# Narrowing float64 weights to float32 inside a fused attention, expert and cosine kernel: two bit operations instead of three, low word through ScalarE and GpSimd

## The chip, the cores and the metric

One core of one Trainium2 chip runs the whole program in one launch. The metric is the time of one execution on the device, in microseconds (us); lower is better. The engines are TensorE (PE; its weight loads are PEld), VectorE (DVE), ScalarE (ACT), GpSimd (POOL) and SyncE (SP), which here only issues transfers. Each engine takes its instructions in the order of the program, and DMA engines move data between device memory and the on-chip memory (SBUF).

## What is computed

```python
# 1: attention over pairs of averaged queries, (4, 8, 1152, 64)
q_pool = q.reshape(B, H, S // 2, 2, D).mean(axis=3)
scores = scale * np.matmul(q_pool, k.transpose(0, 1, 3, 2))
attn = softmax(scores)
x = np.matmul(attn, v)             # then 2304 tokens x 512
# 2: each token goes to one of 8 experts
logits = x @ w_gate
expert_idx = np.argmax(logits, axis=1)
out[mask] = gate_w[mask, None] * (np.maximum(x[mask] @ w1[e], 0.0) @ w2[e])
# 3: a product with a cosine
h = x @ w_in                       # w_in: 512 x 2048, float64
g = h * np.cos(h)
return (g @ w_out).astype(np.float32)   # w_out: 2048 x 512, float64
```

`w_in` and `w_out` arrive as float64, 8 MB each; the engines compute in float32, so the kernel makes float32 copies of them in device memory first. That is the narrowing. A float64 is two 32-bit words: the high word has the sign, 11 bits of exponent and 20 bits of fraction, the low word 32 more bits of fraction.

## The kernel before

The program has three stages that overlap at their ends. The attention stage (to about 640 us) computes 32 heads and routes the tokens. The expert stage works through 12 units of up to 256 tokens, sorted by expert; `Experts.unit` does one. The cosine stage (`Cosine.block`) works through five blocks of up to 512 tokens.

**A unit of the expert stage.** The hidden layer is done in four chunks. For each, TensorE multiplies the tokens with a chunk of `w1` into PSUM (line 916), ScalarE takes the relu into the tile `hh` (line 922), VectorE computes the rounding remainder `hl` from the same PSUM tile (line 923), and TensorE multiplies `hh` and `hl` with a chunk of `w2` (line 955). Products are split in a high and a low part for accuracy. Two chunks are in flight (`HP = 2`). Line 983 scales the unit's result on ScalarE, line 984 copies its row numbers on VectorE. Beside this, weights of later experts are loaded by SP (line 1054), rounded on ScalarE (line 1055) and their remainder taken (line 1056) by VectorE, for the last chunk by GpSimd. GpSimd also issues the gathers of the next units' tokens (lines 1002 and 1010) and of the cosine stage's tokens (line 1030).

**The narrowing.** `Narrow.step` handles 128 rows by 256 columns. There are 64 steps, spread over the first ten units by the table `NSTEP`. A step of the kernel before:

- line 1102, SP: load 256 KB into `raw64`; `hi` and `lo` are its odd and even words;
- line 1108, VectorE: `v` = (hi shifted left by 3) xor a constant;
- line 1109, VectorE: `t` = the sign of hi;
- line 1110, VectorE: `v` = (v and a mask) or `t`;
- line 1112, ScalarE: `t` = hi squared, which says below whether the number is too small;
- line 1113, VectorE: `v` is set to zero where `t` says so;
- line 1114, VectorE: `t` = sign and exponent of `v`, a power of two;
- line 1115, VectorE: `t` = lo times 2 to the -52 times `t`, the low word's share;
- line 1116, GpSimd: `v` = `v` + `t`;
- line 1117, ScalarE's queue: store `v` to `wi_d` or `wo_d` in device memory.

The tiles `raw64`, `v64` and `t64` have four buffers each, so step n + 4 can write a buffer only when step n has read it for the last time. Since `t` is used by lines 1109 and 1110 and then overwritten by line 1112, ScalarE's square has to wait for VectorE's line 1110 of its own step.

**The order.** The code does not fix the order of one step against the rest of its unit: a scheduler orders the instructions of each engine when the program is built, and that order is kept by each engine at run time. An instruction that waits holds up all that follow on its engine.

Of the kernel before, what the change touches and what calls it, by code (L numbers as in the profile page):

```python
# [8 lines left out]
F32 = mybir.dt.float32  # L9
# [4 lines left out]
AF = mybir.ActivationFunctionType  # L14
ALU = mybir.AluOpType
# [17 lines left out]
    l=0.55, v=3.2, vc=2.8, vt=0.3, vx=0.3, n=1.1,  # L33
# [454 lines left out]
class Routing:  # L488
# [83 lines left out]
    def plan(self, at, ends, x, batch, ps, low):  # L572
# [149 lines left out]
        for j, t in enumerate(range(lo, hi)):  # L722
            at(z + 4.4 + j * step, scatter, t)
# [347 lines left out]
class Narrow:  # L1071
# [26 lines left out]
    def step(self, src, dst):  # L1098
        nc, p = self.nc, self.pool
        shape = [P, self.W]  # L1100
        raw = p.tile(shape + [2], I32, name="raw64")
        nc.sync.dma_start(raw, src)
        lo, hi = raw[:, :, 0].bitcast(U32), raw[:, :, 1]
        v = p.tile(shape, I32, name="v64")
        t = p.tile(shape, I32, name="t64")
        vf, tf = v.bitcast(F32), t.bitcast(F32)

        nc.vector.tensor_scalar(v, hi, 3, 0x40000000, op0=ALU.logical_shift_left, op1=ALU.bitwise_xor)
        nc.vector.tensor_single_scalar(t, hi, -0x80000000, op=ALU.bitwise_and)
        nc.vector.scalar_tensor_tensor(v, v, 0x7FFFFFFF, t, op0=ALU.bitwise_and, op1=ALU.bitwise_or)  # L1110

        nc.scalar.activation(tf, hi.bitcast(F32), AF.Square)
        nc.vector.scalar_tensor_tensor(vf, tf, 3.4332275390625e-05**2, vf, op0=ALU.is_ge, op1=ALU.mult)
        nc.vector.tensor_single_scalar(t, v, -0x800000, op=ALU.bitwise_and)
        nc.vector.scalar_tensor_tensor(tf, lo, 2.0**-52, tf, op0=ALU.mult, op1=ALU.mult)
        nc.gpsimd.tensor_add(vf, vf, tf)
        nc.scalar.dma_start(dst, vf)


# [73 lines left out]
def body(ctx, tc, q, k, v, w_gate, w1, w2, w_in, w_out, out):  # L1193
# [104 lines left out]
    with mid as s:  # L1298
# [15 lines left out]
        for u, (i, j, n) in enumerate(UNIT):  # L1314
# [17 lines left out]
            for k in range(NSTEP[u]):  # L1332
                between[k * NCH // NSTEP[u]].append((ORD[2 if u else 3], step))
# [87 lines left out]
```

## Time and profile before

| | |
|---|---|
| median of 3 runs | 1386.64 us (1386.04 to 1390.84) |
| the profiled execution | 1400.46 us, its span 1398.9 us |
| PE busy | 1257.8 us, 90% of the span |
| DVE busy | 1087.6 us, 78% |
| ACT busy | 715.4 us, 51% |
| POOL busy | 626.2 us, 45% |

The profile is of one execution, 1% above the median of the others. Shares over the whole span mix three stages: the narrowing runs only from about 650 to 947 us, so what counts for the change is read from that stretch alone. "Idle before" of a group of instructions is the time for which its engine stood still just ahead of them, and the name behind the arrow is what ended it.

### The profile page before, as it was taken

How to read it: one execution, taken by the hardware profiler on the slowest of the kernel's cores; microseconds unless marked ns; L12 is line 12 of the kernel's file. 1: busy time of each engine (PE TensorE's matmuls, PEld its weight loads, DVE VectorE, ACT ScalarE, POOL GpSimd, SP SyncE). 2: the span in 40 equal slices, each digit the busy share in tenths (PEclk: the TensorE clock that was granted, in tenths of full speed). 3: DMA queues.
4: the chain of work that ended last, by engine and by line, in shares of the span. 5: the costliest groups of instructions: out<-in, count | busy, mean ns of one | idle time of the engine just before them, and what ended most of it. 6: DMA issues, size and time to landing. Idle time of an engine off the chain costs nothing. (4 is left out here: it accounts for less than half of the span.)

```text
span 1398.9 us, 27350 instructions
## 1 busy us (share of the span) xinstructions
PE 1257.8 (90%) x10190; PEld 1059.8 (76%) x10190; DVE 1087.6 (78%) x2203; ACT 715.4 (51%) x1631; POOL 626.2 (45%) x559
## 2 busy tenths in 40 slices
PE   5896997999979999999699897878899999999996
PEld 4686876878868887878588786767687888888885
DVE  5996988788979998865689988796965666667674
ACT  4685875777758876873154334555322223222232
POOL 6684876566668778641354444554302002001010
PEclk8898999799989998999899998999999999999998
DMA  9449345333543342415778767887102001001000
GB/s 173 96 114 183 87 102 73 75 82 86 117 61 93 86 100 63 114 32 98 175 253 251 230 196 242 264 251 220 45 0 63 1 0 61 1 8 38 0 31 16
DMA packets 126910, 146.23 MB, mean 105 GB/s; under 512 B 35888, under 2 KB 83120, under 8 KB 126768
## 3 DMA queue, kind: packets, MB, share of 16 engines
q1 hardware_dynamic: 108784, 114.97, 33.0%
q0 software_dynamic: 5600, 15.25, 3.6%
q10 hardware_dynamic: 12384, 14.17, 3.3%
q8 instruction: 82, 1.34, 0.4%
q14 instruction: 60, 0.49, 0.1%
HBM read 97.57 MB, written 28.43 MB: 90 GB/s over the span
## 5 line engine op out<-in xcount | busy, mean ns | idle before, releaser
L319 POOL TENSOR_TENSOR pl<-pf,ph 128x576 f16<-128x576 f32 x220 | 311.6, 1425 | 138.9 <-ACT ph L309 57.3
L297 ACT ACTIVATE pf<-pst 128x288 f32<-128x288 f32 x576 | 222.5, 419 | 100.5 <-PE pst L289 81.0
L263 DVE TENSOR_REDUCE mm<-pm 128x1 f32<-128x384 f32 x432 | 226.7, 545 | 44.0 <-PE pm L254 36.7
L288 PE MATMUL pst<-q,k 128*128 128x288 f32 x576 | 197.0, 349 | 0.6 <-ACT pf L297 0.4
L289 PE MATMUL pst<-q,k 66*128 66x288 f32 x576 | 173.5, 310 | 25.4 <-DMA q<-mx 25.4
L338 PE MATMUL po<-va,pl 128*128 128x66 f16 (+1 forms) x1440 | 180.3, 198 | 1.8 <-DVE pl L319 1.0
L336 PE MATMUL po<-va,ph 128*128 128x66 f16 (+1 forms) x1440 | 181.7, 199 | 0.2 <-ACT pe L342 0.2
L337 PE MATMUL po<-va,ph 128*128 128x64 f16 (+1 forms) x1440 | 179.4, 197 | 0.0
L482 POOL DMA_INDIRECT out_dram<-os,token x18 | 18.2, 1012 | 353.2 <-ACT os L1186 186.2
L254 PE MATMUL pm<-k,q 128*128 128x384 f32 x384 | 153.3, 418 | 18.1 <-DVE mm L263 14.8
L1157 ACT ACTIVATE a<-a,hpi 128x512 f32<-128x512 f32 (+1 forms) x80 | 54.5, 681 | 210.9 <-DVE a L1156 197.9
L336 PEld LDWEIGHTS <-ph 128*128 128x128 f16 (+1 forms) x1440 | 137.8, 103 | 25.5 <-issue 11.0
L338 PEld LDWEIGHTS <-pl 128*128 128x128 f16 (+1 forms) x1440 | 139.3, 103 | 15.1 <-issue 6.0
L337 PEld LDWEIGHTS <-ph 128*128 128x128 f16 (+1 forms) x1440 | 139.5, 102 | 7.9 <-issue 2.7
L289 PEld LDWEIGHTS pst<-q,k 66*128 66x128 f32 x576 | 114.5, 200 | 27.7 <-DMA q<-mx 18.6
L309 ACT CAST ph<-pf 128x576 f16<-128x576 f32 x191 | 129.5, 680 | 1.4 <-PE po L337 0.4
L1147 PE MATMUL ch<-zh,w1h_m 128*128 128x512 f32 (+1 forms) x320 | 119.6, 374 | 3.5 <-ACTq L1370 3.4
L1147 PE MATMUL ch<-zl,w1h_m 128*128 128x512 f32 (+1 forms) x320 | 119.6, 374 | 0.0
L1147 PE MATMUL ch<-zh,w1l_m 128*128 128x512 f32 (+1 forms) x320 | 119.0, 372 | 0.0
L288 PEld LDWEIGHTS pst<-q,k 128*128 128x128 f32 x576 | 114.1, 199 | 5.8 <-ACT pf L297 2.1
L1171 PE MATMUL po<-w2h_m,gh 128*128 128x512 f32 x288 | 114.2, 396 | 0.0
L1171 PE MATMUL po<-w2l_m,gh 128*128 128x512 f32 x288 | 113.8, 395 | 0.0
(262 smaller groups left out, 3331.6 us busy)
## 6 DMA issues: line engine op xcount, KB each, us to landing
w1r_e<-in_moe_w_dram SPq DMA_DIRECT2D x32, 512.0 KB
w2r_e<-in_moe_w_dram SPq DMA_DIRECT2D x32, 512.0 KB
kr<-in_k_dram SPq DMA_DIRECT2D x32, 288.0 KB
vr<-in_v_dram SPq DMA_DIRECT2D x32, 288.0 KB
k<-k SPq DMA_DIRECT2D x32, 288.0 KB
q<-q SPq DMA_DIRECT2D x60, 144.0 KB
qr<-in_q_dram SPq DMA_DIRECT2D x32, 256.0 KB
raw<-in_moe_w_in_dram SPq DMA_DIRECT2D x32, 256.0 KB
```

The lines of the kernel that those rows point to most:

```text
L254: nc.tensor.matmul(ps[:, :384], self.st[i]["q1"][:, q0 : q0 + P], self.st[i]["k1"][:, ks], start=True, stop=True)
L263: self.nc.vector.tensor_reduce(self.mm[i % 2][:, ci, g : g + 1], self.st[i]["pm", ci, g][:, :384], axis=AX.X, op=ALU.max)
L288: nc.tensor.matmul(ps[:, :288], s["k1"][:, ks], s["q1"][:, o], start=True, stop=False)
L289: nc.tensor.matmul(ps[:, :288], self.k2[i % 3][: D + 2, ks], self.q2[i % 4][: D + 2, o], start=False, stop=True)
L297: nc.scalar.activation(s["pf", c][:, j * 288 : (j + 1) * 288], s["pst", c, j][:, :288], AF.Exp, scale=0.0625)
L309: nc.scalar.copy(ph, pf)
L319: low = eng.tensor_sub(s["pl"][:, c, :], s["pf", c], s["ph"][:, c, :])
L336: nc.tensor.matmul(po[:, :66], hi, va[:, c, D:130], start=(c == 0), stop=False)
L337: nc.tensor.matmul(po[:, :D], hi, va[:, c, :D], start=False, stop=False)
L338: self.product = nc.tensor.matmul(po[:, :66], lo, va[:, c, D:130], start=False, stop=(c == NK - 1))
L1147: nc.tensor.matmul(ph[:, :n], wt[:, c, fs], z[:, c, :n], start=(k == 0), stop=(k == 3 * NDC - 1))
L1171: nc.tensor.matmul(po[j], g[:, ts], wt[:, f % FC, :], start=(f == 0 and k == 0), stop=(f == NFC2 - 1 and k == 2))
```

## The change

Sign and exponent are now made by two operations of VectorE, and `t` is no longer needed there. A new tile `l64`, again with four buffers, takes the low word, scaled by ScalarE; GpSimd multiplies it with the power of two and then adds it. In the changed kernel the lines are: 1108 and 1111 the two bit operations, 1113 the square, 1114 the setting to zero, 1116 the scaling on ScalarE, 1117 the power of two, 1118 the multiplication on GpSimd, 1119 the addition, 1120 the store.

```diff
-        nc.vector.tensor_scalar(v, hi, 3, 0x40000000, op0=ALU.logical_shift_left, op1=ALU.bitwise_xor)
-        nc.vector.tensor_single_scalar(t, hi, -0x80000000, op=ALU.bitwise_and)
-        nc.vector.scalar_tensor_tensor(v, v, 0x7FFFFFFF, t, op0=ALU.bitwise_and, op1=ALU.bitwise_or)
+        nc.vector.tensor_scalar(
+            v, hi, 3, 0x3FFFFFFF, op0=ALU.logical_shift_left, op1=ALU.bitwise_and
+        )
+        nc.vector.scalar_tensor_tensor(v, hi, -0x40000000, v, op0=ALU.bitwise_and, op1=ALU.bitwise_or)
 
         nc.scalar.activation(tf, hi.bitcast(F32), AF.Square)
         nc.vector.scalar_tensor_tensor(vf, tf, 3.4332275390625e-05**2, vf, op0=ALU.is_ge, op1=ALU.mult)
+        l = p.tile(shape, F32, name="l64")
+        nc.scalar.activation(l, lo, AF.Copy, scale=2.0**-52)
         nc.vector.tensor_single_scalar(t, v, -0x800000, op=ALU.bitwise_and)
-        nc.vector.scalar_tensor_tensor(tf, lo, 2.0**-52, tf, op0=ALU.mult, op1=ALU.mult)
-        nc.gpsimd.tensor_add(vf, vf, tf)
+        nc.gpsimd.tensor_mul(l, l, tf)
+        nc.gpsimd.tensor_add(vf, vf, l)
         nc.scalar.dma_start(dst, vf)
```

The scheduler orders the expert stage anew. Three places follow; a number behind a name is only that of a buffer or of an instruction.

VectorE, second unit, before: from the remainder of its first chunk (`hl_u_0`) to that of its second (`hl_u_1`). Line 1108 there begins the fifth step and needs the `v` of the first.

```order
L923 SCALAR_TENSOR_TENSOR hl_u_0_12579<-ph_u_0_12553,hh_u_0_12578 128x512
L1115 SCALAR_TENSOR_TENSOR t_12425<-raw_12422,t_12425 128x256
...
L1115 SCALAR_TENSOR_TENSOR t_12462<-raw_12459,t_12462 128x256
L1109 TENSOR_SCALAR t_12499<-raw_12496 128x256
L1108 TENSOR_SCALAR v_12498<-raw_12496 128x256
L816 TENSOR_REDUCE ext<-ge 128x8
L850 SCALAR_TENSOR_TENSOR seg<-count_u,size 128x12
L923 SCALAR_TENSOR_TENSOR hl_u_1_12608<-ph_u_1_12582,hh_u_1_12607 128x512
```

VectorE, the same place now:

```order
L923 SCALAR_TENSOR_TENSOR hl_u_0_12584<-ph_u_0_12558,hh_u_0_12583 128x512
L818 COPY cum<-ext 128x8
...
L820 TENSOR_TENSOR cum<-cum,ext 128x1
L923 SCALAR_TENSOR_TENSOR hl_u_1_12613<-ph_u_1_12587,hh_u_1_12612 128x512
...
L853 COPY rows<-yx 128x8
L1108 TENSOR_SCALAR v_12502<-raw_12500 128x256
```

The fifth step's first operation has moved from ahead of the second chunk's remainder to behind the third's; only small operations of the routing are left between the first two.

ScalarE, sixth unit, before, from the last weight rounding ahead of its first relu (`hh_u_0`) to its third:

```order
L1055 CAST w2h_e_3_13813<-w2r_e_3_13815 128x1024
...
L1117 DMA wo_d<-v_13465 128x256
L1112 ACTIVATE t_13722<-raw_13719 128x256
L922 ACTIVATE hh_u_0_13914<-ph_u_0_13889 128x512
L922 ACTIVATE hh_u_1_13943<-ph_u_1_13918 128x512
L1117 DMA wo_d<-v_13642 128x256
L1117 DMA wo_d<-v_13655 128x256
L1112 ACTIVATE t_13735<-raw_13732 128x256
L922 ACTIVATE hh_u_2_13972<-ph_u_2_13947 128x512
```

ScalarE, the same place now:

```order
L1120 DMA wo_d<-v_13802 128x256
L983 ACTIVATE ys_u_0_13880<-py_u_0_13545,gate_e_1_13204 128x512
L1116 ACTIVATE l_14031<-raw_14023 128x256
...
L1055 CAST w2h_e_3_13846<-w2r_e_3_13848 128x1024
...
L922 ACTIVATE hh_u_0_13949<-ph_u_0_13924 128x512
L1113 ACTIVATE t_14040<-raw_14037 128x256
L922 ACTIVATE hh_u_1_13978<-ph_u_1_13953 128x512
```

The square and the store that stood right ahead of the unit's first relu are gone from there. A square now depends on its load and on the `t` of four steps before, no longer on VectorE's work in its own step; a scaling (line 1116) depends on its load and on the `l` of four steps before.

GpSimd, around the first gather of the cosine stage's tokens, before (the row ahead of it is the 54th addition):

```order
L1116 TENSOR_TENSOR v_14795<-v_14795,t_14796 128x256
L1030 DMA yg_15672<-y_d,source 128x513
L1056 TENSOR_TENSOR w1l_e_3_15149<-w1r_e_3_15150,w1h_e_3_15148 128x1024
L1032 COPY token<-yg_15672 128x1
L1116 TENSOR_TENSOR v_14832<-v_14832,t_14833 128x256
```

GpSimd, the same place now (the row ahead of the gather is the 64th and last addition):

```order
L1118 TENSOR_TENSOR l_15500<-l_15500,t_15495 128x256
...
L1119 TENSOR_TENSOR v_15494<-v_15494,l_15500 128x256
L1118 TENSOR_TENSOR l_15538<-l_15538,t_15533 128x256
L1119 TENSOR_TENSOR v_15532<-v_15532,l_15538 128x256
L1030 DMA yg_15736<-y_d,source 128x513
L1056 TENSOR_TENSOR w1l_e_3_15208<-w1r_e_3_15209,w1h_e_3_15207 128x1024
```

All 64 steps now lie ahead of that gather on GpSimd, and on ScalarE all 64 stores lie ahead of the first relu of the tenth unit, where 54 did.

## Rows read from the trace of the kernel before

**Rows 1.** Stretches: length; busy us (instructions) of PE, PEld, DVE, ACT, POOL; PE's clock; DMA.

```profile
650.00:905.00 255.00, 218.51 (x1302) 190.86 (x1302) 209.85 (x517) 103.19 (x169) 121.84 (x98) 0.91 0.73 218
905.00:950.00 45.00, 34.60 (x186) 29.37 (x186) 36.58 (x66) 21.34 (x36) 24.21 (x22) 0.89 0.78 244
...
1000.00:1387.00 387.00, 383.60 (x1771) 315.15 (x1770) 261.37 (x467) 109.26 (x182) 28.77 (x36) 1.00 0.06 19
```

**Rows 2.** Chain of work that ended last, its shares of the span by line.

```profile
by line: PE ch L1147 11.3%; PE po L1171 11.2%; PE pt_y L1065 0.3%; POOLq L1417 0.1%; ACTq L1417 0.1%; POOL out_dram L482 0.1%; issue 0.0%; ACT os L1186 0.0%; POOLq L482 0.0%; ACTq L1186 0.0%
```

**Rows 3.** Who waited for whom: PE, 640 to 1000 us (total, times, longest).

```profile
PE py_u L955 <- DVE hl_u L923: 17.7, 9, 4.6
PE py_u L955 <- ACT hh_u L922: 16.9, 4, 7.5
```

**Rows 4.** Groups of instructions, 640 to 950 us: busy us, mean ns | idle before.

```profile
L1116 POOL TENSOR_TENSOR v<-v,t 128x256 f32<-128x256 f32 x64 | 70.3, 1105 | 89.1 <-DVE t L1115 60.7 <-issue 17.0 <-DMA wi_d<-v 3.1
...
L1113 DVE SCALAR_TENSOR_TENSOR v<-t,v 128x256 f32<-128x256 f32 x64 | 39.0, 617 | 4.7 <-ACT t L1112 4.7
L1115 DVE SCALAR_TENSOR_TENSOR t<-raw,t 128x256 f32<-128x256 uint32 x64 | 35.8, 570 | 0.2
...
L1110 DVE SCALAR_TENSOR_TENSOR v<-v,t 128x256 int32<-128x256 int32 x64 | 32.4, 518 | 0.2
...
L1112 ACT ACTIVATE t<-raw 128x256 f32<-128x256 f32 x64 | 27.1, 436 | 96.1 <-DVE v L1110 84.0 <-POOL v L1116 6.5 <-DMA wo_d<-v 5.2
...
L1114 DVE TENSOR_SCALAR t<-v 128x256 int32<-128x256 int32 x64 | 24.1, 385 | 0.0
...
L1109 DVE TENSOR_SCALAR t<-raw 128x256 int32<-128x256 int32 x64 | 20.5, 322 | 10.7 <-DMA raw<-in_moe_w_out_dram 5.8 <-DMA raw<-in_moe_w_in_dram 4.3 <-POOL v L1116 0.6
L1108 DVE TENSOR_SCALAR v<-raw 128x256 int32<-128x256 int32 x64 | 19.3, 307 | 22.6 <-DMA wi_d<-v 13.2 <-DMA wo_d<-v 9.3
```

**Rows 5.** Timeline of GpSimd, VectorE, ScalarE and PE, 786 to 792 us (start, us).

```profile
787.29 2.36 POOL L1056 TENSOR_TENSOR w2l_e<-w2r_e,w2h_e 128x1024 fp32r<-128x1024 f32 x1
...
786.76 3.19 DVE L1113 SCALAR_TENSOR_TENSOR v<-t,v 128x256 f32<-128x256 f32 x1
...
792.48 0.67 DVE L923 SCALAR_TENSOR_TENSOR hl_u<-ph_u,hh_u 128x512 fp32r<-128x512 f32 x1
...
790.31 0.43 ACT L1112 ACTIVATE t<-raw 128x256 f32<-128x256 f32 x1 [4.41 <-DVE v L1110]
...
791.28 0.79 PE L955 MATMUL py_u<-w2h_e,hh_u 128*128 128x512 f32 x1 [5.36 <-ACT hh_u L922]
```

**Rows 6.** Timeline of VectorE and PE, 847 to 853 us.

```profile
847.99 3.85 DVE L1110 SCALAR_TENSOR_TENSOR v<-v,t 128x256 int32<-128x256 int32 x1
...
852.85 0.79 PE L955 MATMUL py_u<-w2h_e,hh_u 128*128 128x512 f32 x1 [7.52 <-ACT hh_u L922]
```

**Rows 7.** Timeline of VectorE and PE, 676 to 678 us.

```profile
676.16 0.33 DVE L1108 TENSOR_SCALAR v<-raw 128x256 int32<-128x256 int32 x1 [5.10 <-DMA wi_d<-v]
...
677.84 0.79 PE L955 MATMUL py_u<-w2h_e,hl_u 128*128 128x512 f32 x1 [4.59 <-DVE hl_u L923]
```

**Rows 8.** A short stretch, columns as in rows 1.

```profile
791.30:796.30 5.00, 4.30 (x9) 2.96 (x10) 4.73 (x14) 0.98 (x3) 2.67 (x3) 0.50 0.64 176
```

**Rows 9.** Who waited for whom: SP's DMA queue, 640 to 960 us.

```profile
SPq L1102 <- DVE t L1115: 97.0, 37, 11.0
```

**Rows 10.** Groups of instructions, 640 to 950 us: rounding of w2 on ScalarE.

```profile
L1055 ACT CAST w2h_e<-w2r_e 128x1024 fp32r<-128x1024 f32 x29 | 30.3, 1046 | 25.2 <-DMA w2r_e<-in_moe_w_dram 13.3 <-POOL v L1116 10.4 <-PE py_u L955 0.9
```

**Rows 11.** Instructions of lines 1116 and 1117: ns min/median/max, first and last start.

```profile
L1116 POOL TENSOR_TENSOR v<-v,t x64: 717/818/4145, 660.2 to 945.1; 128x256 f32<-128x256 f32 x64
...
L1117 ACTq DMA_DIRECT2D wi_d<-v x32: 326/326/451, 661.0 to 879.4; - x32
L1117 ACTq DMA_DIRECT2D wo_d<-v x32: 326/326/358, 749.0 to 946.7; - x32
```

**Rows 12.** Timeline of ScalarE: the first relu of the tenth unit.

```profile
906.95 0.60 ACT L922 ACTIVATE hh_u<-ph_u 128x512 fp32r<-128x512 f32 x1
```

## The prediction

> **What bounds the kernel now.** I read the table by stretches first, to see in which part of the program TensorE stands still. From 1000 us on, in the cosine stage, it is busy 383.6 of 387 us at full clock [rows 1], and the chain of work that ended last is made there of its matmuls alone [rows 2]. So a microsecond by which that stage starts earlier or later moves the end by one. The narrowing runs ahead of it. From 650 to 905 us TensorE is idle for 255 - 218.5 = 36.5 us, from 905 to 950 us for 10.4, and its clock is granted to 0.91 and 0.89 [rows 1]. Those 47 us, with the clock lost around them, are all the change can win at once; VectorE is the fullest of the helpers, 209.9 of 255 us.
>
> Then I asked who ends TensorE's waits: the relu of ScalarE, 16.9 us in 4 waits, and the remainder of VectorE, 17.7 in 9 [rows 3]. Neither is long work; both stand in a queue behind something else. The groups by line say what: ScalarE stood still for 84.0 us ahead of its squares because VectorE had not done line 1110 [rows 4]. The timelines show the coupling at its worst. GpSimd subtracts a weight chunk for 2.36 us; VectorE's line 1113 takes 3.19 us beside it; ScalarE stands 4.41 us ahead of the square, with the relu queued behind it, and TensorE stands for 5.36 us [rows 5]. The same happens at 853 us, with line 1110 held 3.85 us and TensorE 7.52 [rows 6]. At 678 us VectorE itself waits 5.10 us for a free `v`, with a remainder queued behind it: 4.59 us of TensorE [rows 7].
>
> **The change, part by part.** *VectorE.* Line 1109 goes, 64 x 0.322 = 20.6 us, and line 1115, 64 x 0.570 = 36.5 [rows 4]: 57.1 us less. The new second bit operation reads two tiles as line 1110 did, so it stands at 0.518, at nothing net. *ScalarE* gains 64 scalings. The nearest row is the square, same shape, same spacing of the source: 64 x 0.436 = 27.9 us [rows 4], on an engine busy 103.2 of 255 us [rows 1], beside waits that hide it. *GpSimd* gains 64 multiplications. The nearest row is line 1116, of equal shape: 0.717 at least, 1.105 on average, 4.145 at most [rows 4, 11]; I take the mean, 70.7 us. Beside GpSimd's 121.8 of 255 us [rows 1] this has room, but not much (below). The other bit operation and the stores keep their price.
>
> *Waits that go.* (a) At 678 us the remainder now stands ahead of the fifth step, as the second extract in the part on the change shows: 4.6 us gone. (b) The square no longer needs VectorE, so at 791 and 853 us the relu runs early: 5.36 + 7.52 = 12.9 us are at stake. But the remainder, which TensorE needs right after, was itself only done at 793 us [rows 5], on a VectorE that still stops for GpSimd's 2.36. Between nothing and 12.9 I take half, 6.4. (c) From 905 us on no narrowing is left in the new order, where ten stores were still to come: half of the 10.4 us idle there, 5.2; the rest waits for weights. (d) The clock: from 791.3 to 796.3 us, right behind a wait, it was granted at 0.50 (the 1.2 GHz level), and 4.30 us of matmuls [rows 8] would have taken half at the upper level: 2.15 us lost. One such loss for (a), and half of two for (b): 4.3. Together 20.5 us.
>
> *Waits that come.* (e) Stores and scalings on ScalarE's queue both wait for GpSimd. Such waits stood at 10.4 us ahead of the w2 rounding [rows 10] and 6.5 ahead of a square [rows 4]; with twice the work per step on GpSimd I let them double, 16.9 us more of ScalarE. In the new order 13 of 40 relus stand directly behind a store or a scaling (9 before), so 13/40 of it reaches TensorE: 5.5 us, between 0 and 16.9. (f) The narrowing is packed closer: 64 stores ahead of the tenth unit's first relu, at 906.95 us [rows 12], where 54 stood. What is left of the idle time before 905 us, 36.5 - 4.6 - 6.4 = 25.5 us, grows with its density, by 10/54: 4.7 us; it could be none, since SP waited 97.0 us to reload `raw` until line 1115 had read it [rows 9], and the scaling now frees `raw` sooner.
>
> The sum: 20.5 - 5.5 - 4.7 = 10.3 us less. On the profiled execution that is 1400.5 - 10.3 = 1390.2; the median of the runs lies 13.8 us lower, and I take the same difference from it: **1376.3 us**, 0.7% faster. About 0.5%, some 7 us, is what a measurement of this kernel can tell from no change.
>
> **The rivals.** *The wait changes its name (no change).* VectorE's remainder is as late as before, since its long holds come from GpSimd, which now multiplies as well. Then (b) is nothing, (c) too, only (a) and its clock are won: 4.6 + 2.15 - 5.5 - 4.7 = -3.4, so 1390. For it: 17.7 us of TensorE's waits end with the remainder already [rows 3], and the denser order gives VectorE's relief back to the narrowing. Against it: even if each multiplication held VectorE for a whole 0.717, that is 45.9 us, less than the 57.1 it is rid of.
>
> *GpSimd ends last (slower).* In the new order ScalarE cannot take the tenth unit's first relu before all 64 additions, and the first gather of the cosine stage stands behind them on GpSimd. The first store was issued at 661.0 us, the last at 946.7 [rows 11]: 4.5 us a step, where now 3.9 are needed. GpSimd's other work from 650 to 905 us is 121.8 - 54 x 1.105 = 62.2 us [rows 1, 4], so 128 operations have 193 us: the queue is full when their mean reaches 1.5 us. At 1.7 it ends 62.2 + 128 x 1.7 - 255 = 24.8 us late; less (a) and (c), 9.8, the kernel takes 1402, and above a mean of 1.64 it is slower by over 0.5%. For it: the same operation took from 0.717 to 4.145 us [rows 11], and VectorE and GpSimd hold each other up: line 1113 ended 0.3 us after GpSimd's subtraction [rows 5]. Against it: VectorE leaves as many such operations as GpSimd takes up, and 1.105 would have to become 1.5. The Trainium skill (SBUF — State Buffer, "SBUF: two separate sides") speaks for this rival: VectorE and GpSimd share a port pair under an exclusive lock, held for a whole instruction, when VectorE works with two SBUF inputs or in a two-port mode. By that rule the moved multiplication still takes the pair once per step, and the change frees no port time. The trace agrees on the block itself, 3.19 us beside 2.36; that the sum of the holds is the limit no row shows.
>
> **How the numbers follow.** The forecast case has 0.47, with a range of its own from 1363 to 1380: down to all of (b) and (c) with the clock of both waits, 24 us; up to the smallest gain that counts. No change has 0.32, GpSimd last 0.21: the order shows its condition, but only a mean a third higher would meet it. So faster 0.47, same 0.32, slower 0.21. The range for all is 1363 to 1397: below it a tenth or less of the first case, above it somewhat more than half of the last.
>
> **What would show it.** Right: ScalarE's 84 us ahead of the square gone; VectorE's busy time from 650 to 950 us down by 30 us or more; the waits at 791 and 853 us shorter than 3; the last store ahead of 915 us; no narrowing beside units ten to twelve. The first rival: TensorE's wait for the remainder above 20 us while that for the relu falls below 8. The second: lines 1118 and 1119 at 1.5 us or more on average, ScalarE waiting for line 1119 for over 40 us, and the tenth unit's first relu behind 907 us. Wrong altogether: a stop that none of these names, as weights that land late because ten more steps load beside them; ScalarE's 13.3 us for w2 [rows 10] would then grow past 25.

## The result and the profile after

The change makes the kernel slower: 1396.3 us (median of 15 runs, 1392.2 to 1405.6) against 1387.5 for the kernel before beside it, a ratio of 1.0070 with a 95% interval of 1.0048 to 1.0092. The forecast was 1376.3. The profiled execution took 1404.3 us with a span of 1402.7, again one near the top of its runs, so it stands fairly beside that of before (1400.5 and 1398.9).

The stretches of the profile after come first, with the columns of [rows 1]: length, busy time of TensorE, its weight loads, VectorE, ScalarE, GpSimd, then clock and DMA. The second block is the kernel before, from 650 to 950 us.

```profile
650.00:905.00 255.00, 208.83 (x1222) 181.34 (x1221) 210.29 (x424) 122.36 (x227) 171.11 (x167) 0.89 0.75 219
905.00:950.00 45.00, 37.28 (x228) 33.10 (x227) 22.19 (x30) 21.91 (x31) 19.65 (x14) 0.92 0.74 226
1000.00:1391.00 391.00, 387.53 (x1786) 318.01 (x1785) 264.69 (x473) 111.02 (x184) 28.91 (x37) 1.00 0.06 18
...
650.00:950.00 300.00, 246.11 (x1448) 214.43 (x1447) 232.49 (x453) 144.27 (x258) 190.76 (x180) 0.90 0.75 220
```

```profile
650.00:950.00 300.00, 253.12 (x1486) 220.22 (x1486) 246.43 (x583) 124.52 (x203) 146.05 (x119) 0.91 0.74 222
```

The cosine stage is unchanged, full from start to end. From 905 to 950 us TensorE gained 37.28 - 34.60 = 2.7 us, but from 650 to 905 us it lost 218.51 - 208.83 = 9.7, and its clock went from 0.91 to 0.89. The odd number is VectorE's: 128 operations fewer are asked of it in the narrowing, and it is as busy as before, 210.3 against 209.9 us. In part that is because seven more steps lie ahead of 905 us (63 of 64, where 56 did); but over 650 to 950 us, where all the narrowing lies, it is only 13.9 us less busy, where the prediction looked for 30 or more. The groups by line, 640 to 950 us, say why (busy us, mean ns | idle time before and what ended it):

```profile
L1118 POOL TENSOR_TENSOR l<-l,t 128x256 f32<-128x256 f32 x64 | 60.3, 949 | 55.9 <-DVE t L1117 42.1 <-DVE gate_e L1016 4.0 <-ACT w1h_e L1055 3.3
L1119 POOL TENSOR_TENSOR v<-v,l 128x256 f32<-128x256 f32 x64 | 58.4, 921 | 1.9
L1114 DVE SCALAR_TENSOR_TENSOR v<-t,v 128x256 f32<-128x256 f32 x64 | 39.5, 622 | 1.0
L1111 DVE SCALAR_TENSOR_TENSOR v<-raw,v 128x256 int32<-128x256 int32 x64 | 38.6, 610 | 0.5
...
L1117 DVE TENSOR_SCALAR t<-v 128x256 int32<-128x256 int32 x64 | 32.8, 520 | 0.5
...
L1108 DVE TENSOR_SCALAR v<-raw 128x256 int32<-128x256 int32 x64 | 29.7, 470 | 17.2 <-DMA wi_d<-v 9.8 <-issue 3.8 <-POOL l L1118 1.2
...
L1113 ACT ACTIVATE t<-raw 128x256 f32<-128x256 f32 x63 | 27.2, 435 | 62.3 <-POOL l L1118 33.2 <-DMA raw<-in_moe_w_in_dram 16.2 <-DMA raw<-in_moe_w_out_dram 5.5
L1116 ACT ACTIVATE l<-raw 128x256 f32<-128x256 uint32 x63 | 26.7, 432 | 15.9 <-POOL v L1119 14.2 <-issue 1.7
```

Each VectorE operation that stayed got longer. The second bit operation takes 610 ns where line 1110 took 518, the power of two 520 where line 1114 took 385, the first bit operation 470 where line 1108 took 307 [rows 4]. A step's four operations sum to 0.470 + 0.610 + 0.622 + 0.520 = 2.22 us; the six of before summed to 2.72. ScalarE's 84 us of waiting for VectorE's bits are gone, and 33.2 + 14.2 us of waiting for GpSimd have come.

What this does to TensorE, in the waits of 640 to 1000 us (total, times, longest):

```profile
PE py_u L955 <- DVE hl_u L923: 15.5, 6, 8.4
PE py_u L955 <- ACT hh_u L922: 11.2, 5, 3.8
PE py_u L955 <- DVE ys_u L984: 9.8, 3, 5.1
PE pt_e L1065 <- DMA xg_e<-x_d,ix_e: 7.4, 4, 4.3
PE phT_u L944 <- ACT hs_u L938: 6.1, 2, 6.0
```

The copy of line 984 stands next to the remainder on VectorE and feeds no matmul, so its 9.8 us belong to the remainder: 25.3 us, where [rows 3] had 17.7. Of the 25.3, one stop of 8.4 us, at 671 us, is no work of VectorE's that was stretched: VectorE waits there for a store to land. Without it, and without the 4.6 us at 678 us of before [rows 7], where VectorE waited for a store too, the remainder went from 13.1 to 16.9 us. The relu fell from 16.9 to 11.2, gathers and the small units' relu rose from 1.9 and 2.6 before to 7.4 and 6.1. The two waits of before:

```profile
PE phT_u L944 <- ACT hs_u L938: 2.6, 1, 2.6
PE pt_e L1065 <- DMA xg_e<-x_d,ix_e: 1.9, 1, 1.9
```

One of the remainder's waits in full, from the timeline of VectorE, GpSimd and TensorE:

```profile
856.97 0.74 POOL L1119 TENSOR_TENSOR v<-v,l 128x256 f32<-128x256 f32 x1
...
857.06 4.38 DVE L1117 TENSOR_SCALAR t<-v 128x256 int32<-128x256 int32 x1
...
858.24 2.36 POOL L1056 TENSOR_TENSOR w2l_e<-w2r_e,w2h_e 128x1024 fp32r<-128x1024 f32 x1
...
860.54 0.74 POOL L1118 TENSOR_TENSOR l<-l,t 128x256 f32<-128x256 f32 x1
...
861.36 0.68 DVE L923 SCALAR_TENSOR_TENSOR hl_u<-ph_u,hh_u 128x512 fp32r<-128x512 f32 x1
...
862.09 0.80 PE L955 MATMUL py_u<-w2h_e,hl_u 128*128 128x512 f32 x1 [4.38 <-DVE ys_u L984]
```

The power of two needs 0.28 us alone. It was issued while GpSimd added, and ended only when GpSimd had added, subtracted a weight chunk and multiplied: 4.38 us, the remainder right behind it, and TensorE still for 4.38 us. Who is held, and who is not, is plain in two lines' shortest, median and longest times (ns):

```profile
L1117 DVE TENSOR_SCALAR t<-v x64: 277/286/4377, 654.6 to 908.2; 128x256 int32<-128x256 int32 x64
L923 DVE SCALAR_TENSOR_TENSOR hl_u<-ph_u,hh_u x40: 677/682/694, 633.1 to 929.8; 128x512 fp32r<-128x512 f32 x40
```

Line 923, which reads one tile from PSUM and one from SBUF, never took more than 694 ns in this run, whatever GpSimd did. The operations that read SBUF alone are stretched, those with one tile like those with two. The Trainium skill (SBUF — State Buffer, "SBUF: two separate sides") has it so: VectorE with two SBUF inputs, or in a two-port mode, and GpSimd exclude each other on one port pair, for a whole instruction. The trace agrees (which mode line 1117 ran in no row tells), and shows one thing more, that the one who waits can be passed over by several of the other's instructions in a row.

To compare kernels I count this **hold**: over 650 to 950 us, each narrowing operation and weight subtraction on VectorE that the timeline lists singly and that lies beside a tensor operation of GpSimd, its duration less what it takes alone (0.285 us with one tile read, 0.415 with two, 1.22 for a weight chunk, near the medians of such lines). Rows that the timeline merges into one are left out, so it is a count from below. Before it is 39.6 us in 110 instructions, after 59.3 in 145. Outside such company the same operations come to 2.2 us over their time alone at most, in sum, in any of the kernels here.

### The profile page after: what moved, and what is told of

It reads as the page before. It is cut to its first block, busy times and chain, and to the rows that moved or that the text cites. A ratio compares the mean times of both kernels' runs of the same rounds, so it can differ in the third digit from the quotient of the medians.

```text
span 1402.7 us, 27424 instructions
## 1 busy us (share of the span) xinstructions
PE 1254.3 (89%) x10190; PEld 1056.0 (75%) x10190; DVE 1071.0 (76%) x2075; ACT 738.3 (53%) x1695; POOL 673.4 (48%) x623
## 3 DMA queue, kind: packets, MB, share of 16 engines
q1 hardware_dynamic: 108784, 114.97, 33.1%
## 5 line engine op out<-in xcount | busy, mean ns | idle before, releaser
L338 PEld LDWEIGHTS <-pl 128*128 128x128 f16 (+1 forms) x1440 | 138.2, 102 | 15.1 <-issue 5.8
```

The source lines that it names most:

```text
L338: self.product = nc.tensor.matmul(po[:, :66], lo, va[:, c, D:130], start=False, stop=(c == NK - 1))
```

## The experiments

Theories: **A**, VectorE is held by GpSimd's additional work; **B**, raw tiles come free earlier and their loads collide with the units' transfers; **C**, ScalarE waits for GpSimd. All runs together:

| kernel | us | ratio to before (95%) | hold, us |
|---|---|---|---|
| before | 1387.5 | 1 | 39.6 |
| the change | 1396.3 | 1.0070 (1.0048, 1.0092) | 59.3 |
| e1_bits | 1383.1 | 0.9944 (0.9916, 0.9972) | 35.3 |
| e2_low | 1396.2 | 1.0033 (1.0008, 1.0058) | 53.5 |
| e3_dvemul | 1386.8 | 0.9963 (0.9934, 0.9992) | 28.7 |
| e4_nomul | 1389.6 | 0.9993 (0.9965, 1.0022) | 36.5 |
| e5_wdve | 1389.3 | 0.9987 (0.9968, 1.0006) | 39.3 |
| e6_mul2 | 1414.5 | 1.0164 (1.0132, 1.0197) | 74.5 |
| e7_raw3 | 1399.0 | 1.0062 (1.0039, 1.0085) | 54.2 |
| e8_adddve | 1367.7 | 0.9833 (0.9800, 0.9866) | 21.2 |
| e9_idlepool | 1399.0 | 1.0088 (1.0054, 1.0121) | 54.0 |
| e10_handoff | 1396.8 | 1.0048 (1.0018, 1.0078) | 16.8 |
| e11_bits_dve | 1378.0 | 0.9923 (0.9895, 0.9950) | 24.2 |
| e12_before_dve | 1374.0 | 0.9904 (0.9872, 0.9935) | 24.1 |
| e13_five | 1393.5 | 1.0040 (1.0023, 1.0058) | 61.1 |
| e14_hand5 | 1378.2 | 0.9917 (0.9891, 0.9943) | 26.0 |
| e15_dve5 | 1374.1 | 0.9908 (0.9874, 0.9942) | 17.5 |
| e16_dve_w | 1370.8 | 0.9859 (0.9831, 0.9887) | 3.4 |

The kernel before was run beside each group of four and had medians of 1387.5 to 1391.1, so kernels of different groups are compared by their ratios. Through the table the ratio rises with the hold, from 0.986 at 3.4 us to 1.016 at 74.5. A straight line through the other seventeen misses none of them by more than 0.8% and e10_handoff by 1.6%; its slope is 0.6 us of time for 1 us of hold, an estimate from these rows.

**The halves.** e1_bits is the kernel before with the two bit operations alone:

```diff
-        nc.vector.tensor_scalar(v, hi, 3, 0x40000000, op0=ALU.logical_shift_left, op1=ALU.bitwise_xor)
-        nc.vector.tensor_single_scalar(t, hi, -0x80000000, op=ALU.bitwise_and)
-        nc.vector.scalar_tensor_tensor(v, v, 0x7FFFFFFF, t, op0=ALU.bitwise_and, op1=ALU.bitwise_or)
+        nc.vector.tensor_scalar(
+            v, hi, 3, 0x3FFFFFFF, op0=ALU.logical_shift_left, op1=ALU.bitwise_and
+        )
+        nc.vector.scalar_tensor_tensor(v, hi, -0x40000000, v, op0=ALU.bitwise_and, op1=ALU.bitwise_or)
```

> Theories. A (the shared pair of ports): GpSimd's new multiplication holds VectorE's remaining operations, so the remainder is as late as before and VectorE's stretch 650 to 905 us stays at 210 us. B (earlier reloads): the raw tile comes free sooner, so its loads run beside the units' stores, token gathers and weights, and TensorE waits for these. C (ScalarE waits on GpSimd): the squares and scalings that wait for t and l (33 + 14 us) hold the relu and the weight casts. This run is the bit half alone; the low word stays with VectorE and GpSimd has one addition, so nothing of A, B or C is in it: all three expect no loss, 1378 to 1388 us beside 1387.5 before, VectorE's busy time in 650 to 905 us down by 20 us or more. If it is above 1392, all three fall and the cause lies in the order of the steps that the shorter VectorE work brings.

Measured 0.6% faster, as all three had it, with the hold at 35.3 us; only VectorE's busy time did not fall (208.5 us), since more of the narrowing now lies in that stretch. The other half by itself, e2_low, has the three bit operations and the new low word:

```diff
-        nc.vector.scalar_tensor_tensor(tf, lo, 2.0**-52, tf, op0=ALU.mult, op1=ALU.mult)
-        nc.gpsimd.tensor_add(vf, vf, tf)
+        l = p.tile(shape, F32, name="l64")
+        nc.scalar.activation(l, lo, AF.Copy, scale=2.0**-52)
+        nc.gpsimd.tensor_mul(l, l, tf)
+        nc.gpsimd.tensor_add(vf, vf, l)
```

> The low-word half alone: three bit operations on VectorE, the scaling on ScalarE, the multiplication and addition on GpSimd. A: the loss is here, 1394 to 1404 us, and VectorE's busy time in 650 to 905 us goes above 210 us (64 operations more than in the full change). B: here as well, 1392 to 1400, with waits for token gathers as after. C: here as well. If it is within 1384 to 1390, the loss comes only from both halves together.

It is slower, and its hold is 53.5 us. The loss sits in the low word's half; VectorE's busy time did rise, to 212.9. The halves do not add up: -0.6% and +0.3% make -0.2%, where the change has +0.7%. The order of the queues differs in each of the three, and what that is worth comes below.

**GpSimd's multiplication.** In e3_dvemul it goes to VectorE, in e4_nomul it is left out, in e6_mul2 it is there twice; the rest is the change.

```diff
-        nc.gpsimd.tensor_mul(l, l, tf)
+        nc.vector.tensor_mul(l, l, tf)
```

> The full change but the multiplication on VectorE, so that GpSimd has one addition a step as before and t is freed by VectorE. A: the loss goes, 1380 to 1389 us; the bit operations L1108 and L1111 and the power of two L1117 fall back to 0.31, 0.52 and 0.39 us on the mean. B: the raw tile is free as early as in the change, so the loss stays, 1393 to 1399. C: the squares no longer wait for GpSimd, most of the loss goes, 1382 to 1390, whatever VectorE's means are.

```diff
-        nc.gpsimd.tensor_mul(l, l, tf)
         nc.gpsimd.tensor_add(vf, vf, l)
```

> The full change with GpSimd's multiplication left out (the scaled low word is added without its power of two). A: 1376 to 1388 us and VectorE's busy time in 650 to 905 us 20 us or more below the 210 of the change. B: the raw tile is free as early as in the change, so 1392 to 1398 with the same waits for gathers and stores. C: 1380 to 1388, with ScalarE's wait on GpSimd (33 + 14 us) under 20.

```diff
         nc.gpsimd.tensor_mul(l, l, tf)
+        nc.gpsimd.tensor_mul(l, l, tf)
         nc.gpsimd.tensor_add(vf, vf, l)
```

> The change with a second GpSimd multiplication of the same size in each step (the low word is multiplied twice, so its value differs). From no multiplication to one, the time went from 1389.5 to 1396 us. A: the dose goes on, another 6 to 14 us: 1402 to 1412, time of VectorE beside GpSimd above 75 us over its time alone. B: the raw tile comes free no earlier and no later, so 1394 to 1400. C (ScalarE waits for GpSimd): also longer, 1402 to 1415, but then with ScalarE's wait on GpSimd going from 47 us to over 80 while VectorE's time beside GpSimd stays near 60.

No multiplication on GpSimd 0.9993, one 1.0070, two 1.0164: each costs 0.8 to 0.9%, some 11 to 13 us. The groups by line of e4_nomul, then of e6_mul2, between which GpSimd's two multiplications are the whole difference:

```profile
L1111 DVE SCALAR_TENSOR_TENSOR v<-raw,v 128x256 int32<-128x256 int32 x64 | 33.8, 535 | 0.3
```

```profile
L1111 DVE SCALAR_TENSOR_TENSOR v<-raw,v 128x256 int32<-128x256 int32 x61 | 50.6, 836 | 0.7
...
L1113 ACT ACTIVATE t<-raw 128x256 f32<-128x256 f32 x60 | 26.1, 436 | 54.7 <-POOL l L1119 49.5 <-DVE v L1114 2.3 <-DVE hl_u L923 2.2
L1116 ACT ACTIVATE l<-raw 128x256 f32<-128x256 uint32 x58 | 24.4, 433 | 38.5 <-POOL v L1120 33.1 <-DVE xl_e L1068 3.2 <-issue 2.0
```

The bit operation goes from 535 over 610 to 836 ns on VectorE, while its hold goes 36.5, 59.3, 74.5. The hold missed its mark of 75 by a hair, but ScalarE's waits for GpSimd grew as well, to 49.5 + 33.1 us, so the dose does not part A from C; e9_idlepool below does. B is out as the main cause: in e3_dvemul and e4_nomul the raw tile is free as early as in the change, and they are not slower than before. In e3_dvemul the three means fell to 0.38, 0.53 and 0.37 us, the first not as far as A had said; in e4_nomul VectorE's busy time fell to 186.3, as it had.

**Fewer loads ahead**, e7_raw3, tests B itself, and **less other work on GpSimd**, e5_wdve, tests A without touching the steps.

```diff
-        raw = p.tile(shape + [2], I32, name="raw64")
+        raw = p.tile(shape + [2], I32, name="raw64", bufs=3)
```

> The change with three raw tiles instead of four, so that a step's load is issued one step later and fewer loads stand beside the units' stores and gathers; no engine's work changes. B: most of the loss goes, 1385 to 1391 us, and TensorE's waits for token gathers (7.4 us) and the wait for the store of the first unit (13.5 us on VectorE) go. A: 1394 to 1402, not better, since VectorE is held as before.

```diff
-        ws[i].append(weight_chunk(nc, wp[i % 2], wp["raw"], w1[number[i]], w2[number[i]], c, f"e{i}_{c}", (c == NCH - 1 and (i > 0 or E0P),) * 2))
+        ws[i].append(weight_chunk(nc, wp[i % 2], wp["raw"], w1[number[i]], w2[number[i]], c, f"e{i}_{c}", (False,) * 2))
```

> The change with the weights' subtractions of each last chunk on VectorE instead of GpSimd. A (VectorE is held beside GpSimd's work; in the change its five narrowing and subtraction groups spend 60 us more beside it than alone): GpSimd loses 34 us of work in 650 to 905 us, VectorE gains 14 x 1.22 = 17 us of its own, the time beside GpSimd falls below 45 us: 1388 to 1396 us. B (earlier reloads collide with the units' transfers): untouched, 1394 to 1400. If VectorE's own amount of work sets the time, 1398 to 1406.

e7_raw3 is no faster than the change, though TensorE's waits for gathers fell from 7.4 to 3.3 us and VectorE's longest wait for a unit's store from 13.5 to 2.4: B falls. e5_wdve, where a step passes through GpSimd as in the change, is back within the error of before, 0.8% faster than the change, with 20 us less hold although VectorE took on 14 weight subtractions. GpSimd's busy time fell by only 16 us there (171.1 to 155.3), since steps moved up into the stretch.

**Nothing of the step on GpSimd**, e8_adddve:

```diff
-        nc.gpsimd.tensor_mul(l, l, tf)
-        nc.gpsimd.tensor_add(vf, vf, l)
+        nc.vector.tensor_mul(l, l, tf)
+        nc.vector.tensor_add(vf, vf, l)
```

> The change with the multiplication and the addition both on VectorE, so that GpSimd has nothing of a step but its gathers and weights. A: VectorE's time beside GpSimd falls to 15 us over its time alone or less, against 64 x 0.42 = 27 us of additions that it takes on: about even with the multiplication alone on VectorE (1386.8), 1380 to 1390. If VectorE's own amount of work sets the time, as the prediction had it, 10 to 20 us above that run: 1394 to 1406.

1367.7 us, faster than both kernels and than either theory allowed; the hold, at 21.2 us, is above the 15 that A had said. Six operations a step on VectorE, and TensorE is busy 227.1 of 255 us, as the groups by line and the stretch show:

```profile
L1111 DVE SCALAR_TENSOR_TENSOR v<-raw,v 128x256 int32<-128x256 int32 x64 | 33.3, 528 | 0.0
L1114 DVE SCALAR_TENSOR_TENSOR v<-t,v 128x256 f32<-128x256 f32 x64 | 30.7, 485 | 0.0
...
L1118 DVE TENSOR_TENSOR l<-l,t 128x256 f32<-128x256 f32 x64 | 28.0, 446 | 0.0
L1119 DVE TENSOR_TENSOR v<-v,l 128x256 f32<-128x256 f32 x64 | 27.5, 436 | 0.1
...
L1117 DVE TENSOR_SCALAR t<-v 128x256 int32<-128x256 int32 x64 | 22.6, 362 | 0.0
L1108 DVE TENSOR_SCALAR v<-raw 128x256 int32<-128x256 int32 x64 | 18.3, 292 | 13.0 <-DMA wi_d<-v 10.6 <-DMA wo_d<-v 1.8 <-issue 0.4
```

```profile
650.00:905.00 255.00, 227.07 (x1377) 200.24 (x1376) 217.66 (x549) 138.51 (x247) 74.55 (x46) 0.93 0.83 247
```

The six take 2.55 us a step, the change's four 2.22: two operations more, 0.33 us more.

**Load or hand-off?** e8_adddve takes away GpSimd's load and the step's way through GpSimd together. Two kernels put one of them back each. e9_idlepool adds load whose result nobody reads, e10_handoff the way without the load:

```diff
+        d = p.tile(shape, F32, name="d64", bufs=1)
+        for _ in range(2):
+            nc.gpsimd.tensor_mul(d, l, l)
-        nc.vector.tensor_mul(l, l, tf)
-        nc.vector.tensor_add(vf, vf, l)
+        nc.vector.tensor_mul(tf, l, tf)
+        nc.vector.tensor_add(vf, vf, tf)
```

> The multiplication and addition on VectorE (1367.7 us), and beside them two GpSimd multiplications of the same size in each step whose result nobody reads, into a tile of its own. Theory A is split. A1 (sharing): GpSimd's tensor operations stretch VectorE's whatever hangs on them: 1382 to 1398 us, VectorE's groups beside GpSimd 35 us or more over their time alone. A2 (hand-offs): it is the step's passing through GpSimd, with ScalarE and the store waiting for it, that costs: nothing waits here, so 1365 to 1374.

```diff
+        nc.gpsimd.tensor_copy(tf[:, :1], tf[:, :1])
         nc.vector.tensor_mul(l, l, tf)
         nc.vector.tensor_add(vf, vf, l)
+        nc.gpsimd.tensor_copy(vf[:, :1], vf[:, :1])
```

> The multiplication and addition on VectorE, but the step still passes through GpSimd twice: a one-column copy of t onto itself ahead of the multiplication and of v ahead of the store. A1: GpSimd's operations are too short to stretch much: 1365 to 1376 us. A2: the two hand-offs of the change are all there, 1382 to 1398.

Each alone brings the loss back, 1.0088 and 1.0048. They do it in different ways. In e9_idlepool, 1 us above the range of A1, the hold is 54.0 us; TensorE's waits, from 640 to 1000 us, are for the most part for the remainder (19.7 us in e8_adddve). One thing does wait for the idle load, ScalarE's next scaling into the same `l`, but only for 3.4 us:

```profile
PE py_u L955 <- DVE hl_u L923: 42.9, 9, 7.4
...
ACT l L1116 <- POOL d L1120: 3.4, 2, 2.7
...
PE py_u L955 <- ACT hh_u L922: 0.4, 2, 0.2
```

So the loss comes back while ScalarE hardly waits for GpSimd and TensorE hardly waits for the relu: C is not needed for a loss of this size, and A is enough.

In e10_handoff the hold is 16.8, the smallest but one. VectorE waits for the stores that free a step's `v` for 18.8 + 1.1 us (10.6 + 1.8 in e8_adddve), and TensorE has two long stops that e8_adddve lacks, for a remainder at the head of the cosine stage and for a token gather:

```profile
DVE v L1108 <- DMA wi_d<-v: 18.8, 11, 4.2
...
PE pt_y L1065 <- DVE zl L1068: 14.2, 1, 14.2
...
PE pt_e L1065 <- DMA xg_e<-x_d,ix_e: 9.5, 1, 9.5
...
DVE v L1108 <- DMA wo_d<-v: 1.1, 2, 0.8
```

Together they are 23.7 us, where the profiled spans, 1400.2 and 1369.4, differ by 30.8. Such stops come without any hand-off as well: 13.5 us for that remainder in e16_dve_w, 12.2 and 18.4 us for a gather in e11_bits_dve and e15_dve5.

Whether that way acts by holding the four sets of tiles longer, and how much of it is in the change, is what a fifth set tells. The edit is the same in the change (e13_five), in e10_handoff (e14_hand5) and in e8_adddve (e15_dve5):

```diff
-        nw = ns.enter_context(tc.tile_pool(name="nw", bufs=4, side="right", reuse_waits="tile"))
+        nw = ns.enter_context(tc.tile_pool(name="nw", bufs=5, side="right", reuse_waits="tile"))
```

> The change with five sets of the step's tiles instead of four. A1 (sharing): VectorE's operations are held as before, 1393 to 1402 us. A2 (hand-offs, by holding the four sets longer): a fifth set covers the longer step, 1378 to 1389, and VectorE's waits for the stores (9.8 us) and ScalarE's waits for GpSimd (47 us) halve.

> The kernel with two one-column hand-offs (1396.8 us) with five sets of tiles. If the hand-offs act by holding the sets: 1370 to 1385, and VectorE's waits for the stores of wi_d, 18.8 us with four sets, fall below 10. If they act by the order of the queues (an operation of GpSimd stands behind another whose input is late): 1390 to 1402.

> Control: the multiplication and addition on VectorE (1367.7 us) with five sets of tiles. Nothing waits for the sets there but the first operation of a step (12.4 us for stores): 1362 to 1370 by either theory. If it is above 1375, a fifth set costs something of its own and the two runs beside it have to be read against this one.

The fifth set gives the hand-off kernel back 1.3% (1.0048 to 0.9917), to where its control stands (0.9908). Its VectorE waits 6.5 us for `wi_d` in place of 18.8, as was said for holding sets, but 8.6 for `wo_d` in place of 1.1, so for stores 15.1 us in place of 19.9:

```profile
DVE v L1108 <- DMA wo_d<-v: 8.6, 5, 4.9
...
DVE v L1108 <- DMA wi_d<-v: 6.5, 4, 2.7
```

Both long stops are gone too, and the last store is issued at 933 us in place of 966. So a fifth set repays the two hand-offs; that they cost by holding sets fits this, but is not shown, since a new order of the queues can remove such stops as well. In the change the fifth set gives 0.3%, less than the two intervals can part, with a hold of 61.1 us, and ScalarE's waits for GpSimd did not halve (20.2 + 17.8 us). VectorE's waits for the stores of `wi_d` did, from 9.8 to 2.3 us, and that bought next to nothing: there the load is the larger cause. The control was above its range, 1362 to 1370, if not above 1375. It lost 0.75% by the fifth set, with one stop that no theory names, in TensorE's waits:

```profile
PE pt_e L1065 <- DMA xg_e<-x_d,ix_e: 23.1, 3, 18.4
```

The scheduler orders every queue anew for each edit, and a gather that lands late can be worth that much. Differences below 0.8% between single edits are not to be read one by one here.

**What is left.** e11_bits_dve and e12_before_dve are e1_bits and the kernel before with only the addition moved to VectorE; e16_dve_w is e8_adddve with the edit of e5_wdve.

```diff
-        nc.gpsimd.tensor_add(vf, vf, tf)
+        nc.vector.tensor_add(vf, vf, tf)
```

> Two bit operations, the low word in one VectorE operation as before (no scaling on ScalarE), and the addition on VectorE: six VectorE operations a step as in the run at 1367.7, 64 scalings of 0.43 us less on ScalarE. A: ScalarE was not the bound, so 1362 to 1370. If ScalarE's 28 us of scalings held the relus and casts, 1350 to 1361.

> The kernel before with nothing changed but the addition, which moves from GpSimd to VectorE: seven VectorE operations a step, 64 x 0.42 = 27 us more VectorE work than before and 70 us less on GpSimd. A: the 40 us that VectorE spent beside GpSimd over its time alone goes for the most part, 1368 to 1380 us. If VectorE's own amount of work sets the time, 1395 to 1410.

> The multiplication and addition on VectorE, and the weights' subtractions of each last chunk too, so that GpSimd has no tensor operation left between 650 and 905 us. A1: the 21 us that VectorE's groups still spend beside GpSimd over their time alone fall below 8, against 14 x 1.22 = 17 us of subtractions that VectorE takes on: 1362 to 1373 us, even within its error. If VectorE's amount of work is now the bound: 1374 to 1384.

The kernel before gains 1.0% by one word: VectorE gets a seventh operation of 0.44 us and the sum of its step rises only from 2.72 to 2.96 us, the hold falling from 39.6 to 24.1. Without GpSimd in the step the third bit operation is worth nothing that can be measured (0.9904 with it, 0.9923 without). e11_bits_dve missed its mark: a step has six VectorE operations as in e8_adddve and less ScalarE work, and it is 0.9% behind, with one wait of 12.2 us for a gather; whether ScalarE's scaling helps is left open. e16_dve_w has next to no hold, 3.4 us, and is even with e8_adddve. VectorE's 14 subtractions (17 us) are one place where the gain can have gone, the stop of 13.5 us at the head of the cosine stage, which e8_adddve does not have, is another; which of them it is stays open.

## Why the prediction was wrong

The view was right in what it took for the limit: TensorE's idle time from 650 to 950 us moves the end, and it did. The sign was wrong, by the steps below. That 1396.3 us still lies in the range for all, 1363 to 1397, is luck: its upper end came from the second rival, whose mechanism did not happen.

- **VectorE rid of 57.1 us: wrong, the step that failed.** The prediction let "the other bit operation and the stores keep their price", took the second bit operation "at nothing net" and priced GpSimd's multiplication on GpSimd alone, 70.7 us for which there was room; what 64 more operations there do to VectorE's stands at nothing in the sum. Four operations at 2.22 us against six at 2.72 are 0.50 us a step, 31.8 us in 64 steps. The other 25.3 us came back as longer times of the four that stayed, 0.40 us a step, and the hold rose from 39.6 to 59.3 us. Of the gains, (b) and its half of (d), 6.4 + 2.15 of the 20.5 us, rested on the freer VectorE, and among the losses there was no term for a VectorE that is held longer. e3_dvemul prices it closest: with the multiplication on VectorE its five operations take 0.383 + 0.532 + 0.485 + 0.372 + 0.500 = 2.27 us, so moving it to GpSimd rids VectorE of 0.05 us a step, about 3 us in all, and gives GpSimd 64 x 0.949 = 60.7. The forecast against its first rival ("even if each multiplication held VectorE for a whole 0.717, that is 45.9 us, less than the 57.1") set a hold against a price that was itself partly hold: line 1115's 0.570 us is a mean, its median is 0.417.
- **(a) The stop at 678 us: gone, and replaced.** A stop of 8.44 us stands at 671 us; there the remainder is behind the copy of line 984, which waited for a unit's store to land. This is no hold, and e8_adddve, the fastest kernel, has the like (8.16 us at 667 us):

```profile
670.59 0.15 DVE L984 COPY ys_u<-ix_u 128x1 f32<-128x1 f32 x1 [13.47 <-DMA y_d<-ys_u]
...
670.74 0.68 DVE L923 SCALAR_TENSOR_TENSOR hl_u<-ph_u,hh_u 128x512 fp32r<-128x512 f32 x1
...
671.48 0.79 PE L955 MATMUL py_u<-w2h_e,hl_u 128*128 128x512 f32 x1 [8.44 <-DVE hl_u L923]
```

- **(b) Half of 12.9 us: nothing.** The relu did get early, as said, and the square no longer waits for VectorE's bits. But stops of 5.05 us at 798 and 4.38 at 862 us came with the remainder late behind a held operation.
- **(c) 5.2 us from 905 us on: 2.7.** The last store was issued at 912 us, as the order showed.
- **(d) The clock, 4.3 us: not won;** from 650 to 905 us it was granted at 0.89 where it had 0.91, with TensorE busy 9.7 us less.
- **(e) ScalarE's waits for GpSimd:** they came, 33.2 + 14.2 us, but not on the relus, whose share of TensorE's waits fell to 11.2 us. 5.5 us was too much at that place.
- **(f) Denser packing, 4.7 us:** gathers rose by 5.5 us and the small units' relu by 3.5. In e7_raw3, where a step's load is issued later, both are lower again (3.3 and 3.5 us) and the time is the same, so the loss does not hang on them.

The first rival, "the wait changes its name", had the mechanism: the remainder ends TensorE's waits, above 20 us, though 8.4 of the 25.3 us are the stop at 671 us; at 798 and 862 us GpSimd held what stood ahead of it. The relu's 11.2 stayed over its mark of 8, and its price of no change was too kind, since it kept the 57.1. Of the second rival's marks one was met, the tenth unit's first relu behind 907 us (917.4). But lines 1118 and 1119 took 0.95 and 0.92 us, not 1.5, ScalarE waited for line 1119 for less than 40 us, and GpSimd was busy 171 of 255 us. GpSimd did not end last; it slowed its neighbour. The rule of the Trainium skill (SBUF — State Buffer, "SBUF: two separate sides") that stood beside that rival belonged to the first, and the sentence that no row showed the sum of the holds as the limit was where to go on: the rows by line had it in part, as means of 0.518 to 0.617 us against medians of 0.416 and 0.417.

What stays open: how much of the change's own 0.7% is hold and how much the chance order of its queues. That GpSimd's load costs is shown by the dose (none, one, two multiplications), by e5_wdve and by e9_idlepool. That the step's way through GpSimd can cost when four sets are all there is, e10_handoff and e14_hand5 suggest; whether it is the tiles or the order of the queues that costs there is open.

## What to carry to other kernels

In this kernel an elementwise operation that reads SBUF alone was not taken off VectorE by giving it to GpSimd beside it. Compare a group's mean with its shortest time: the difference was, here, what GpSimd already cost. Here the best place for both operations was VectorE itself, 1.7% faster than before (e8_adddve), and one moved addition gave the kernel before 1.0%. Where a step passes through one more engine, try one more set of tiles, with a control: the fifth set gave 1.3% back to the kernel with hand-offs and cost the one without them 0.75%.

## What was not expected of the hardware

An operation that waits for its turn may be passed over repeatedly. In e8_adddve, where GpSimd has only weights, gathers and index loads, the bit operation of 0.42 us took 6.05 us, through two weight subtractions with an index load between them, as the timelines of VectorE and of GpSimd show:

```profile
821.52 6.05 DVE L1111 SCALAR_TENSOR_TENSOR v<-raw,v 128x256 int32<-128x256 int32 x1
827.50 0.68 DVE L1068 TENSOR_TENSOR xl_e<-pt_e,xh_e 128x512 fp32r<-128x512 f32 x1
```

```profile
820.93 0.95 POOL L1010 DMA_INDIRECT xg_e<-x_d,ix_e  x1 [0.30 <-issue]
821.91 2.40 POOL L1056 TENSOR_TENSOR w1l_e<-w1r_e,w1h_e 128x1024 fp32r<-128x1024 f32 x1
824.26 0.59 POOL L1002 DMA_DIRECT2D ix_e<-idx_d  x1
824.88 2.40 POOL L1056 TENSOR_TENSOR w2l_e<-w2r_e,w2h_e 128x1024 fp32r<-128x1024 f32 x1
```

It began before the first subtraction and ended 0.3 us after the second.
